# An expert stage's second product: one PSUM tile for both halves of a slot, or one for each

## The chip, the cores and the metric

The kernel runs on one core of a Trainium2 chip. The metric is the device time of one execution in microseconds (us). The engines of a core are TensorE (PE, matmuls; its weight loads are shown as PEld), VectorE (DVE), ScalarE (ACT), GpSimd (POOL) and SyncE (SP). Matmuls write to PSUM, ACT and DVE read it from there into SBUF, DMAs move data between SBUF and device memory (HBM).

## The reference

The input is first filtered along the sequence by a Fourier transform, then goes through a three-way maxout layer, and at last through a layer of eight experts of which each token uses one:

```python
# 1: filter
X = np.fft.rfft(x, axis=1); y = np.fft.irfft(X * F, n=3072, axis=1)     # x: (8, 3072, 256)
# 2: maxout, on 24576 tokens of 256 numbers, inner width 768
x = np.maximum(np.maximum(y @ w1, y @ w2), y @ w3) @ w_out
# 3: experts, inner width 1024
logits = xn @ en.T / tau;  expert_idx = np.argmax(logits, axis=1)        # 8 experts
for e in range(E):
    mask = expert_idx == e
    h = np.maximum(x[mask] @ w1[e], 0.0)
    out[mask] = gate_w[mask, None] * (h @ w2[e])
```

The change touches the last line alone, `h @ w2[e]` and the multiplication by the gate.

## The kernel before

All matmul operands are split into a high and a low part (`split`), and each product is the sum of three matmuls (high by high, high by low, low by high), so that the sum is near float32. `mm` (L214) issues every such matmul.

The program has two parts that follow each other. In the first, up to about 2115 us, filter and maxout run interleaved; its results (`pso` from `x2_tile`, evicted in three ACT instructions on L579 to L585) go to HBM as the table `x2d`, and each token's place in a list by expert is written (`route1` to `route3`).

In the second part, the expert stage, the lists are cut into *slots* of 256 tokens, all of one expert. 103 slots are built, of which the first 100 run in the generator `slots` and the last three stand in a branch that is taken only if they are needed; with this input 100 run. For each slot `s`:

- `w_load` (L1061) fetches the expert's weights into one of three buffers (`w` stands for two of them, `wt` for the third), an indirect DMA on POOL's queue; rows of an expert that is there already are skipped. `x_load` (L1106, POOL's queue) gathers the tokens three slots ahead, `x_turn` (L1118, SP's queue) transposes them by DMA, and `x_split` makes `xT`: two copies (ACT L1126, DVE L1127), then the high part on ACT (L217) and the low part on DVE (L218).
- `up(s, j)`, `j` from 0 to 3, is a quarter of the first product: two of the eight blocks of 128 inner features, 6 matmuls of 256 columns a block, 12 in all, into a PSUM tile `psh` of a pool of five. ACT makes `h`'s high part (L1148), DVE its low part (L1149).
- `down(s, t)`, `t` 0 and 1, is the second product for the first or second 128 tokens of the slot: 24 matmuls into `pso3` (shown as `pso`), over all eight blocks of `h`. Then ACT multiplies by the gate and evicts to `o` (L1165).
- `o_store(s)` scatters the two halves of `o` to the output (L1170, POOL's queue).

The order on every engine is that in which the code issues (a manual schedule; no scheduler moves anything). `slots` goes through its steps so: up(s,0), up(s,1), down(s-1,0), x_split(s+1), up(s,2), down(s-1,1), then the output's stores and the loads and transposes for later slots, up(s,3). So 12 matmuls of the first product stand between the two halves of the second, and 36 between the second half and the next slot's first half. The last step has no `up`: there the two halves of the last slot follow each other directly.

`pso3` comes from the PSUM pool `pf` (L231) with three buffers, each of one bank (2 KB a partition); that pool also serves the filter and the routing. One tile of 2 by 256 float32 fills a buffer. The build makes an instruction wait for an earlier one on another engine if both use the same tile and one writes.

Of the kernel before, what the change touches and what calls it, by code (L numbers as in the profile page):

```python
# [10 lines left out]
F32 = mybir.dt.float32  # L11
# [5 lines left out]
ACTF = mybir.ActivationFunctionType  # L17
# [3 lines left out]
NB, SEQ, D = 8, 3072, 256  # L21
# [161 lines left out]
def fft_filter_maxout_moe_kernel(ctx: ExitStack, tc: tile.TileContext, I, out):  # L183
# [4 lines left out]
    pe, act, dve, pool, sp = nc.tensor, nc.scalar, nc.vector, nc.gpsimd, nc.sync  # L188
# [24 lines left out]
    def mm(o, l, r, start, stop):  # L213
        pe.matmul(out=o, lhsT=l, rhs=r, start=start, stop=stop)  # L214
# [5 lines left out]
    def body():  # L220
        st = ExitStack()
        with st:
            def mk(name, bufs, **kw):
                return st.enter_context(tc.tile_pool(name=name, bufs=bufs, **kw))
# [3 lines left out]
            m1_p, m2_p, h_p = mk("m1", 2), mk("m2", 2), mk("h", 8)  # L228
            mk("gap", 1).tile([128, 32], F32, name="gap")
            gs_p, r_p, rt_p = mk("gs", 2), mk("r", 1), mk("rt", 2)  # L230
            pp, pf = mk("pp", 5, space=PSUM), mk("pf", 3, space=PSUM)  # L231
# [560 lines left out]
            for j in range(2):  # L792
                for k in range(2):
                    for w in range(3):
                        key = (w, k, j)
                        sc = slice(WM * 384 * j, WM * 384 * (j + 1))
                        c = slice(384 * j, 384 * j + 384)
# [300 lines left out]
            xg, xT, hs, ot = {}, {}, {}, {}  # L1098
# [32 lines left out]
            def parts(s, i):  # L1131
                t = ws[BUF[s]][i]
                return (
                    t.rearrange("p (a c d) -> p a c d", a=2, c=8) if i
                    else t.rearrange("p (a k c m) -> p a k c m", a=2, k=2, c=8)
                )
# [16 lines left out]
            def down(s, t):  # L1153
                w, g = parts(s, 1), gates[s]
                if t == 0:
                    ot[s] = (
                        m1_p.tile([128, 2, D], F32, tag="m1", name="o"),
                        pf.tile([128, 2, D], F32, tag="pf", name="pso3"),
                    )
                o, ps = ot[s]  # L1160
                for f in range(8):
                    h = hs[s, f // 2]
                    for i, (a, c) in enumerate(((0, 0), (0, 1), (1, 0))):
                        mm(ps[:, t], h[:, a, f % 2, 128 * t:128 * t + 128], w[:, c, f], f + i == 0, f == 7 and i == 2)
                act.activation(out=o[:, t], in_=ps[:, t], func=ACTF.Copy, scale=g[:, t].bitcast(F32))  # L1165

            def o_store(s):
                o = ot.pop(s)[0]
                for t in range(2):
                    d = pool.indirect_dma_start(  # L1170
                        out=out, out_offset=bass.IndirectOffsetOnAxis(ap=slot[s][:, t], axis=0),
                        in_=o[:, t], in_offset=None, bounds_check=NTOK - 1, oob_is_err=False,
                    )
                    tc.declare_no_dep(d.ins, group="out", reason="every row is written once")
                    tc.add_to_no_dep_group("out", d.ins)

            def slots(first, end):

                for s in range(first, end + 1):
                    on, near = s < end, first < s < end - 1  # L1180
                    if s == first:
                        w_load(AFTER.get(s - 1, 4), 0)
                        w_load(AFTER.get(s - 1, 4), 1)
                    for j in range(4):
                        if on:
                            up(s, j)
                        if j in (1, 2):
                            if on:
                                yield
                            if s > first:  # L1190
                                down(s - 1, j - 1)
                        if j == 1 and near:
                            x_split(s + 1)
                        if j == 2:
                            if s > first:
                                o_store(s - 1)
                            if s + 2 < end:
                                x_turn(s + 2)
                            if s + 3 < end:
                                x_load(s + 3)  # L1200
                            if s > first and AFTER.get(s - 1, end) < end:
                                w_load(AFTER[s - 1], 1)
                        if j == 3 and AFTER.get(s, end) < end:
                            w_load(AFTER[s], 0)
                        yield
# [40 lines left out]
            for x in range(18 * 49):  # L1246
                u, pt = divmod(x, 18)
                fc, w = divmod(pt, 3)
# [101 lines left out]
```

## Time and profile before

| what | us |
|---|---|
| three runs | 3310.49, 3314.74 (median), 3317.52 |
| the profiled execution, its own time | 3308.4 |
| its span, first to last instruction | 3306.6 |
| PE busy in the span | 3176.2 (96%) |
| last matmul starts, last eviction starts | 3295.77, 3296.09 |

The profiled execution's time is 1.8 us more than its span. A busy time of PE counts a matmul from its start to its modelled end, and matmuls overlap, so a busy PE is not one at its peak. A name such as `pso` stands for the tile with the buffer's number left out; times in a timeline count from the span's start.

### The profile page before, as it was taken

The numbers are of one execution on the slowest core, as the hardware profiler recorded it, in microseconds if no ns is written. First come the engines' busy times: TensorE is split into PE (matmuls) and PEld (weight loads), VectorE is DVE, ScalarE is ACT, GpSimd is POOL, SyncE is SP. The second block draws the span as 40 slices with busy tenths as digits, with TensorE's granted clock in tenths as the row PEclk, the third lists the DMA queues.
The fourth block names the chain that finished last, engine by engine and source line by source line (L and its number), as shares of the span: only waits on it lengthen the run. The fifth ranks groups of instructions, "written<-read, shape, count | busy, mean of one in ns | idle before, by whom it ended". The sixth has DMA issues, their size and how long they took to land.

```text
span 3306.6 us, 57241 instructions
## 1 busy us (share of the span) xinstructions
PE 3176.2 (96%) x20524; PEld 2842.3 (86%) x20524; DVE 1920.5 (58%) x4313; ACT 1525.4 (46%) x3450; POOL 1252.1 (38%) x1310
## 2 busy tenths in 40 slices
PE   5899999999999999999999999989999999999998
PEld 2588888888888888888888878889999999999998
DVE  6678687786788756878657675433333333333332
ACT  3455555556555554554446554333333333333333
POOL 3233233232333322333222233255555555555553
PEclk6799999999999999999999999999999999999999
DMA  7756566566555442444217865324233445224234
GB/s 233 220 146 146 141 140 138 136 121 159 139 116 119 89 138 79 99 104 98 54 35 229 214 198 187 95 60 120 69 69 71 118 118 170 68 68 118 70 70 141
DMA packets 345346, 405.61 MB, mean 123 GB/s; under 512 B 169240, under 2 KB 253475, under 8 KB 342116
## 3 DMA queue, kind: packets, MB, share of 16 engines
q1 hardware_dynamic: 248756, 247.81, 31.8%
q0 software_dynamic: 55088, 103.76, 10.7%
q10 hardware_dynamic: 41216, 50.35, 4.7%
q8 instruction: 164, 2.69, 0.4%
q14 instruction: 122, 1.00, 0.1%
HBM read 613.61 MB, written 140.97 MB: 228 GB/s over the span
## 4 chain that ended last, share of the span: by engine, by line
PE 34%; issue 21%; POOL 14%; DVE 2%; DMA 1%; POOLq 1%; ACT 0%; another core or an unknown queue 0%; SPq 0%; ACTq 0%; DVEq 0%
PE p L214 22%; PE pso L214 8%; POOL out L1170 5%; POOL xg L1106 4%; POOL w L1061 4%; POOL wt L1061 2%; PE psy L214 1%; PE psi L214 1%; PE psb L214 1%; DMA gt<-s 1%; PE psa L214 1%; DMA xw<-xg 0%; POOLq L1170 0%; POOLq L1106 0%; POOLq L1061 0%
## 5 line engine op out<-in xcount | busy, mean ns | idle before, releaser
L214 PE MATMUL p<-y,wt 128*128 128x512 f32 x5184 | 1306.9, 396 | 6.4 <-DVE m L553 3.9
L214 PEld LDWEIGHTS p<-y,wt 128*128 128x128 f32 x5184 | 952.8, 189 | 200.0 <-DVE m L553 4.1
L1149 DVE SCALAR_TENSOR_TENSOR h<-psh,h 128x512 fp32r<-128x512 f32 x400 | 275.7, 689 | 408.5 <-ACT h L1148 277.1
L214 PEld LDWEIGHTS pso<-wo,h 128*128 128x128 f32 x3456 | 448.5, 190 | 19.8 <-ACT m L545 3.6
L214 PE MATMUL pso<-wo,h 128*128 128x264 f32 x3456 | 454.0, 286 | 3.2 <-ACT m L545 3.2
L214 PE MATMUL pso<-w,h 128*128 128x256 f32 x3264 | 410.8, 282 | 12.2 <-ACT o L1165 9.3
L214 PE MATMUL psh<-xT,w 128*128 128x256 f32 x3264 | 410.8, 280 | 8.7 <-DMA w<-wsd,wi 4.4
L214 PEld LDWEIGHTS pso<-w,h 128*128 128x128 f32 x3264 | 391.6, 189 | 24.4 <-ACT o L1165 24.4
L214 PEld LDWEIGHTS psh<-xT,w 128*128 128x128 f32 x3264 | 394.2, 190 | 10.2 <-issue 8.3
L398 POOL TENSOR_TENSOR t<-t,ft 96x256 f32<-96x256 f32 (+1 forms) x192 | 185.2, 966 | 557.8 <-issue 256.6
L1170 POOL DMA_INDIRECT out<-o,ti x200 | 200.8, 1004 | 448.9 <-ACT o L1165 440.0
L1148 ACT ACTIVATE h<-psh 128x512 fp32r<-128x512 f32 x400 | 237.3, 594 | 282.0 <-PE psh L214 252.6
L523 POOL TENSOR_TENSOR y<-df,sm 128x256 fp32r<-128x256 f32 x192 | 156.8, 817 | 485.8 <-DVE df L522 477.4
L676 POOL DMA_INDIRECT lst<-ids,pi x192 | 214.5, 1117 | 325.8 <-DVE gs L260 147.9
L1165 ACT ACTIVATE o<-pso,gate 128x256 f32<-128x256 f32 x200 | 94.8, 474 | 442.5 <-PE pso L214 434.0
L259 ACT ACTIVATE h<-m 128x512 fp32r<-128x512 f32 x288 | 181.4, 630 | 218.5 <-DVE m L553 200.6
L218 DVE TENSOR_TENSOR xT<-xf,xT 128x512 fp32r<-128x512 f32 x100 | 69.2, 692 | 363.7 <-ACT xT L217 291.6
L260 DVE TENSOR_TENSOR h<-m,h 128x512 fp32r<-128x512 f32 x288 | 210.7, 732 | 70.7 <-ACT h L259 67.0
L553 DVE TENSOR_TENSOR m<-p,m 128x512 f32<-128x512 f32 x288 | 197.4, 685 | 87.2 <-PE p L214 82.5
L549 DVE TENSOR_TENSOR m<-p,m 128x512 f32<-128x512 f32 x288 | 197.0, 684 | 72.1 <-PE p L214 63.0
L579 ACT COPY r<-pso 128x512 uint16<-128x512 uint16 x192 | 112.5, 586 | 259.0 <-PE pso L214 238.1
L1106 POOL DMA_INDIRECT xg<-x2d,ti x200 | 205.7, 1029 | 67.2 <-issue 62.9
(176 smaller groups left out, 4192.5 us busy)
## 6 DMA issues: line engine op xcount, KB each, us to landing
ft<-in_filt SPq DMA_DIRECT2D x192, 192.0 KB
wsd<-wsp SPq DMA_DIRECT2D x32, 1024.0 KB
x2d<-r SPq DMA_DIRECT2D x48, 514.0 KB
xt<-in_x SPq DMA_DIRECT2D x96, 256.0 KB
s<-ot ACTq DMA_DIRECT2D x96, 256.0 KB
gt<-s SPq DMA_DIRECT2D x94, 256.0 KB
bt<-bmd SPq DMA_DIRECT2D x320, 72.0 KB
raw<-in_e SPq DMA_DIRECT2D x32, 512.0 KB
```

Source lines behind the costliest of these rows:

```text
L214: pe.matmul(out=o, lhsT=l, rhs=r, start=start, stop=stop)
L259: act.activation(out=hi, in_=src, func=ACTF.Copy)
L260: later(1, lambda: dve.tensor_tensor(out=lo, in0=src, in1=hi.bitcast(F32), op=ALU.subtract))
L398: pool.tensor_tensor(out=t[:, w], in0=t[:, w], in1=by(ft, 1), op=ALU.mult)
L549: dve.tensor_tensor(out=m2, in0=ps, in1=m_t[u, fc], op=ALU.max)
L553: dve.tensor_tensor(out=m2, in0=ps, in1=m2, op=ALU.max)
L676: s = pool.indirect_dma_start(out=lst1, out_offset=bass.IndirectOffsetOnAxis(ap=pi[:, t:t + 1], axis=0), in_=ids[:, t:t + 1], in_offset=No ...
L1061: pool.indirect_dma_start(out=ws[BUF[s]][i].bitcast(F32), out_offset=None, in_=wsd[i], in_offset=bass.IndirectOffsetOnAxis(ap=cols["wi"][: ...
L1106: pool.indirect_dma_start(out=g[:, t], out_offset=None, in_=x2d[0:n], in_offset=bass.IndirectOffsetOnAxis(ap=slot[s][:, t], axis=0), bound ...
L1148: act.activation(out=h[:, 0], in_=ps, func=ACTF.Relu)
L1149: dve.scalar_tensor_tensor(out=h[:, 1], in0=ps, scalar=0.0, in1=h[:, 0].bitcast(F32), op0=ALU.max, op1=ALU.subtract,)
L1170: d = pool.indirect_dma_start(out=out, out_offset=bass.IndirectOffsetOnAxis(ap=slot[s][:, t], axis=0), in_=o[:, t], in_offset=None, bounds ...
```

## The change

Each call of `down` takes a tile of its own of 256 float32 from the pool, where before the first call took one of 2 by 256 for both calls. The output tile `o` in SBUF remains one for both.

```diff
             def down(s, t):
                 w, g = parts(s, 1), gates[s]
                 if t == 0:
-                    ot[s] = (
-                        m1_p.tile([128, 2, D], F32, tag="m1", name="o"),
-                        pf.tile([128, 2, D], F32, tag="pf", name="pso3"),
-                    )
-                o, ps = ot[s]
+                    ot[s] = m1_p.tile([128, 2, D], F32, tag="m1", name="o")
+                o = ot[s]
+                ps = pf.tile([128, D], F32, tag="pf", name="pso3")
                 for f in range(8):
                     h = hs[s, f // 2]
                     for i, (a, c) in enumerate(((0, 0), (0, 1), (1, 0))):
-                        mm(ps[:, t], h[:, a, f % 2, 128 * t:128 * t + 128], w[:, c, f], f + i == 0, f == 7 and i == 2)
-                act.activation(out=o[:, t], in_=ps[:, t], func=ACTF.Copy, scale=g[:, t].bitcast(F32))
+                        mm(ps, h[:, a, f % 2, 128 * t:128 * t + 128], w[:, c, f], f + i == 0, f == 7 and i == 2)
+                act.activation(out=o[:, t], in_=ps, func=ACTF.Copy, scale=g[:, t].bitcast(F32))
 
             def o_store(s):
-                o = ot.pop(s)[0]
+                o = ot.pop(s)
```

The pool's buffers keep their size, since its other tiles are of 2 by 256. A slot now takes two of the three in turn instead of one.

On PE, in a slot late in the stage, the end of the first half, the first product's third quarter and the second half stood so before (numbers tell tiles apart: `pso_38306` is the slot's output tile, the `h` are its four inner tiles):

```order
L214 MATMUL pso_38306<-w_21263,h_38267 128x256 x3
L214 MATMUL psh<-xT,w_24599 128x256 [waits PE_49]
L214 MATMUL psh<-xT,w_24599 128x256 x11
L214 MATMUL pso_38306<-w_21263,h_38140 128x256 [waits Activation_49]
L214 MATMUL pso_38306<-w_21263,h_38140 128x256 x5
L214 MATMUL pso_38306<-w_21263,h_38156 128x256 x6
L214 MATMUL pso_38306<-w_21263,h_38207 128x256 x6
L214 MATMUL pso_38306<-w_21263,h_38267 128x256 x6
```

and stand so in the changed kernel:

```order
L214 MATMUL pso_38392<-w_21263,h_38353 128x256 x3
L214 MATMUL psh<-xT,w_24599 128x256 [waits PE_49]
L214 MATMUL psh<-xT,w_24599 128x256 x11
L214 MATMUL pso_38442<-w_21263,h_38225 128x256 x6
L214 MATMUL pso_38442<-w_21263,h_38241 128x256 x6
L214 MATMUL pso_38442<-w_21263,h_38292 128x256 x6
L214 MATMUL pso_38442<-w_21263,h_38353 128x256 x6
```

The matmuls stand in the same order; the second half writes another tile, and its first matmul no longer waits for ACT.

On ACT, from the first half's eviction to the second's, another slot near the end, before:

```order
L1165 ACTIVATE o<-pso_39620,gate 128x256 [waits DMASW5_49,DMASW4_49,PE_49]
L1126 COPY xf<-xw 128x2x2x128 [waits DMAHW7_49,DMAHW0_49]
L217 ACTIVATE xT<-xf 128x512 [waits DVE_49,Activation_49]
L1148 ACTIVATE h_39667<-psh 128x512 [waits PE_49]
L1165 ACTIVATE o<-pso_39620,gate 128x256 [waits PE_49]
```

and in the changed kernel, where the eviction's line is L1163:

```order
L1163 ACTIVATE o<-pso_39715,gate 128x256 [waits DMASW5_49,DMASW4_49,PE_49]
L1126 COPY xf<-xw 128x2x2x128 [waits DMAHW7_49,DMAHW0_49]
L217 ACTIVATE xT<-xf 128x512 [waits DVE_49,Activation_49]
L1148 ACTIVATE h_39762<-psh 128x512 [waits PE_49]
L1163 ACTIVATE o<-pso_39765,gate 128x256 [waits PE_49]
```

Here nothing moved and no wait changed; the second eviction reads another tile than the first.

## Rows read from the trace of the kernel before

**Rows 1.** The page: PE's busy share of 40 slices, and the granted clock.
```profile
PE   5899999999999999999999999989999999999998
PEclk6799999999999999999999999999999999999999
```

**Rows 2.** Busy time of each engine by stretch.
```profile
core 0: us, PE busy (x) PEld busy (x) DVE busy (x) ACT busy (x) POOL busy (x), PEclk, DMA share, GB/s
1100.00:1300.00 200.00, 200.00 (x1086) 171.50 (x1085) 120.50 (x279) 105.03 (x256) 46.70 (x55) 1.00 0.40 110
2135.80:2140.80 5.00, 5.00 (x26) 5.00 (x25) 0.69 (x1) 0.64 (x2) 1.64 (x2) 0.50 0.85 120
2300.00:2500.00 200.00, 196.88 (x1655) 193.54 (x1655) 65.25 (x120) 78.02 (x138) 104.26 (x104) 1.00 0.29 68
2500.00:2700.00 200.00, 196.27 (x1650) 192.93 (x1650) 65.83 (x121) 77.46 (x138) 104.60 (x104) 1.00 0.43 110
```

**Rows 3.** All waits of PE from 2190 us: total us, times, longest.
```profile
PE pso L214 <- ACT o L1165: 14.9, 55, 0.6
```

**Rows 4.** Tile pso, whole span: durations in ns, and who waited for it.
```profile
L214 PEld LDWEIGHTS pso<-w,h x3264: 186/188/330, 2121.6 to 3295.7; 128*128 128x128 f32 x192
...
L1165 ACT ACTIVATE o<-pso,gate x200: 468/474/477, 2124.9 to 3296.1; 128x256 f32<-128x256 f32 x100
...
  PEld pso L214: 37.0, 93
```

**Rows 5.** Timeline of two slots: start and length in us, [idle before <-releaser].
```profile
2501.72 2.99 PE L214 MATMUL pso<-wt,h 128*128 128x256 f32 x24
...
2504.55 1.54 PE L214 MATMUL psh<-xT,w 128*128 128x256 f32 x12
2505.70 0.47 ACT L1165 ACTIVATE o<-pso,gate 128x256 f32<-128x256 f32 x1 [3.18 <-PE pso L214]
...
2506.22 2.81 PEld L214 LDWEIGHTS pso<-wt,h 128*128 128x128 f32 x24 [0.33 <-ACT o L1165]
2506.22 3.01 PE L214 MATMUL pso<-wt,h 128*128 128x256 f32 x24
...
2507.53 0.69 DVE L218 TENSOR_TENSOR xT<-xf,xT 128x512 fp32r<-128x512 f32 x1 [3.85 <-ACT xf L1126]
...
2509.07 4.41 PE L214 MATMUL psh<-xT,w 128*128 128x256 f32 x36
...
2513.31 2.99 PE L214 MATMUL pso<-w,h 128*128 128x256 f32 x24
...
2516.14 1.54 PE L214 MATMUL psh<-xT,w 128*128 128x256 f32 x12
...
2517.81 3.10 PE L214 MATMUL pso<-w,h 128*128 128x256 f32 x24
...
2520.74 1.54 PE L214 MATMUL psh<-xT,w 128*128 128x256 f32 x12
...
2522.12 2.88 PE L214 MATMUL psh<-xT,wt 128*128 128x256 f32 x24
...
2524.84 2.99 PE L214 MATMUL pso<-w,h 128*128 128x256 f32 x24
```

**Rows 6.** Timeline, start of one second half: its first weight loads and matmuls.
```profile
2517.80 0.77 PEld L214 LDWEIGHTS pso<-w,h 128*128 128x128 f32 x6 [0.32 <-ACT o L1165]
2517.81 0.86 PE L214 MATMUL pso<-w,h 128*128 128x256 f32 x5
```

**Rows 7.** Timeline of the stage's end.
```profile
3282.81 1.11 PE L214 MATMUL pso<-w,h 128*128 128x256 f32 x8
...
3283.76 1.54 PE L214 MATMUL psh<-xT,w 128*128 128x256 f32 x12
3283.96 0.47 ACT L1165 ACTIVATE o<-pso,gate 128x256 f32<-128x256 f32 x1 [2.23 <-PE pso L214]
...
3285.14 2.99 PE L214 MATMUL pso<-w,h 128*128 128x256 f32 x24
...
3292.95 2.90 PEld L214 LDWEIGHTS pso<-w,h 128*128 128x128 f32 x24 [0.82 <-ACT o L1165]
```

## The prediction

> **What bounds the kernel now.** I read the page first. TensorE (PE) is busy 96% of the span and the granted clock stands at nearly full speed in almost every slice [rows 1], so time can only be won where PE stands still or spaces its matmuls wider. The change touches only the expert stage, the last third of the span. There the table by stretches shows PE busy 196 to 197 of each 200 us at granted clock 1.00, while VectorE (DVE) has work for 65, ScalarE (ACT) for 78 and GpSimd (POOL) for 104 us [rows 2]: PE is the bound and the others have room. A slot holds 96 matmuls of 256 columns (48 of the first product, 48 of the second); 1655 + 1650 of them in 400 us make 0.1210 us each, 11.62 us a slot.
>
> Next I asked what PE waits for in that stage. From 2190 us to the end the list of its waits has a single line: `pso`, the second product's output, waits for the ACT instruction `o` on L1165, which evicts that output [rows 3]. That line is small (14.9 us) because a PE row counts as idle only after the modelled end of the last matmul. The weight loads, which stand in the same queue, show it in full: 93 idle times before a `pso` load, 37.0 us, ended by `o` [rows 4].
>
> The timeline shows where. At 2501.72 the first half's 24 matmuls begin, at 2504.55 twelve `psh` matmuls of the next slot, and at 2505.93 (12 by 0.115) the second half should begin. It begins at 2506.22, its weight load after 0.33 us of idle time ended by `o` [rows 5]. That `o` evicts the *first* half; it reads other columns of the same PSUM tile, and the build orders the second half behind it.
>
> One more thing is to be seen. `o` takes 0.47 us [rows 4] and would be done long before the twelve matmuls are. But it starts only at 2505.70, although the first half's last matmul ends, as modelled, at 2504.71: 1.0 us late. In the last `slots` step that computes both products, where no gather, transpose or weight load for a later slot is issued any more, `o` starts at 3283.96, 0.04 us after the first half's end (3282.81 + 1.11), and the second half begins at 3285.14, 12 spacings behind 3283.76, with no idle time [rows 7]. So the late start, not the eviction's length, makes PE wait; why it is late the trace doesn't say.
>
> **The change, part by part.** *Removed:* the wait of each second half on the first half's eviction. The instruction order shows the twelve `psh` matmuls followed by the second half with no wait; nothing else on PE, and no instruction or DMA on any engine, moves.
>
> Price of one wait. Matmuls are spaced 0.118 us (2501.72 to 2504.55, 24 of them) [rows 5]. A weight load lasts 0.188 us [rows 4] and so normally overlaps the next by 0.07. A mean stop is (37.0 - 0.82) / 92 = 0.393 us of idle time, the 0.82 being the last slot's [rows 4, 7]; with the lost overlap, 0.464 us. The matmul rows agree: at 2517.81 the gap to the last `psh` (which starts 0.28 before 2516.14 + 1.54) is 0.41, 0.29 too long, and five matmuls then take 0.86 where 4 by 0.118 + 0.28 = 0.75 are normal, 0.11 more, since the second one waits for its weights; 0.40 together, against 0.32 + 0.07 for that slot's load [rows 5, 6].
>
> 92 stops by 0.464 are 42.7 us, and the last slot, where the two halves follow each other directly, gives 0.82 + 0.07. Sum: 43.6 us.
>
> Here a rule could shrink the price. The Trainium skill ("TensorE: Matmul & The Clock Gate", section "Architectural detail: the array is 16× 32×32, not 1× 128×128") says that PE's queue can pull a weight load ahead of matmuls in flight. By it the waiting half's weights would already be in, a stop would cost only the matmul's 0.35 us, and the sum would be 33 us. The trace disagrees: load and matmul start together at 2506.22.
>
> *A side effect on spacing.* Two spacings occur. The 36 `psh` matmuls from 2509.07 take 4.24 us (0.118); those from 2520.74 take 4.10, the 24 from 2522.12 at 0.113 [rows 5]. Behind an unstopped first half at 0.118 the `psh` matmuls go over to the shorter one (twelve from 2516.14: 1.54 - 0.28 over 11, 0.1145). If the second half runs unstopped like the first (2.83 us) and the 36 behind it like those of 2520.74, half and 36 take 6.93 us; now they take 7.09 (2506.22 to 2513.31) or 7.03 (2517.81 to 2524.84), while the delay of the first matmul is 0.464 - 0.11 = 0.35. That makes 0.45 to 0.51 a slot, 41 to 47 us in all. I take 45 us. Bounds: everything at 0.118 gives 96 by 0.118 = 11.33 against 11.62, 0.29 by 92, 27 us; everything at 0.113 gives 10.85, 71 us.
>
> *Added:* a second buffer per slot from a ring of three. The first half's tile is handed out again three halves later, to the next slot's second half: eviction over at 2506.17, next write at 2517.81 [rows 5]. That is 11.6 us of cover; if an eviction were later than this, PE would stop again. Cost: nothing.
>
> *What is late next.* With 0.46 us less per slot, the nearest input of PE is the next slot's `xT`: its low part is written by DVE at 2507.53 for 0.69 and is first read by the first product 12 spacings after 2509.07, at 2510.48 [rows 5]. 2.2 us are spare now, about 1.8 after. The late `o` stays, but only the store on POOL waits for it, and POOL is half empty [rows 2]. Expert weights and gathered rows come by DMA; PE waits for none after 2190 [rows 3], and the stage gets 4% shorter around them.
>
> Sum against the profiled execution: 3308.4 - 45 = 3263.4 us. It ran 6.3 us under the median of the runs shown (3314.74), so for a median I say 3269 us.
>
> **Rivals.**
> 1. *The long spacing stays everywhere.* For it: after a stop the half sometimes runs at once at the short one (3.01 - 0.11 us for 24 from 2506.22), so stops may be one way into it. Against: the unstopped 2520.74 shows the short one too. Gain 27 us: 3288.
> 2. *The wait moves to another input* (`xT`, weights, the ring), or the second half keeps its wait because both tiles count as one. For it: the order of the rows is fixed, and each is needed once a slot. Against: the spare times above, and the order of the changed kernel, which shows the wait gone. Gain near nothing: 3315.
> 3. *Slower: the granted clock falls*, now that PE never pauses. At clock 0.50 (2135.80 to 2140.80, the 1.2 GHz level) 26 matmuls take 5 us, 0.19 each against 0.118 [rows 2], though some records may be missing. Each one at the lower level costs about 0.08 us; some 560 of them, six slots' worth, use up the 45 us. From there on it decides; nine slots' worth gives 3339. Against: from 1100 to 1300 PE is busy 200 of 200 us at clock 1.00 [rows 2].
> 4. *The short spacing spreads:* up to 71 us, say 60: 3254.
>
> **How the numbers follow.** Forecast 0.75 (3260 to 3278, the price bounds of 36 to 50 us and a few us between runs); rival 1 0.12; rival 2 0.05; rival 3 0.03; rival 4 0.05. The range 3256 to 3288 leaves out rivals 2 and 3, and part of rival 4. About 0.2%, 6.6 us, is what a measurement of this kernel can tell from no change: faster 0.92, same 0.05, slower 0.03.
>
> **What would show it.** Right: in the changed profile no PE wait on L1163's `o` after 2190; no weight load idle before `pso`; about 4% more matmuls in 200 us of that stage (some 1720); `o` of the first half still 1 us behind its matmuls; the same tail behind the last matmul, earlier by the sum. Wrong: 48 `psh` matmuls per slot all at 0.118 (rival 1); a new line in PE's waits of some 0.4 us per slot (rival 2); a clock under 1.00 between 2200 and 3200 (rival 3). A gain far off with none of these would mean that the stops overlap something I haven't seen.

## The result, and the profile after

The changed kernel takes 3262.33 us (median of 4 runs, 3259.17 to 3274.65) where the kernel before takes 3312.61 us (4 runs, 3309.33 to 3317.52): a ratio of 0.9852, 95% interval 0.9833 to 0.9872. The profiled execution took 3259.17 us, its span is 3257.3 us.

The page of the changed kernel, PE's busy share and the granted clock in 40 slices, as in [rows 1]:

```profile
PE   5799999999999999999999999989999999999998
PEclk6799999999999999999999999989999999999999
```

The table by stretches, as in [rows 2]:

```profile
core 0: us, PE busy (x) PEld busy (x) DVE busy (x) ACT busy (x) POOL busy (x), PEclk, DMA share, GB/s
2300.00:2500.00 200.00, 200.00 (x1727) 200.00 (x1726) 68.65 (x126) 81.52 (x144) 109.14 (x108) 1.00 0.34 72
2500.00:2700.00 200.00, 200.00 (x1727) 200.00 (x1726) 68.89 (x126) 81.51 (x144) 108.98 (x108) 1.00 0.46 113
```

All waits of PE from 2190 us to the end, as in [rows 3]:

```profile
PE psh L214 <- DVE xT L218: 0.3, 1, 0.3
PE psh L214 <- ACT xT L217: 0.2, 1, 0.2
```

The tile `pso`, as in [rows 4]; no line for PE or its weight loads stands any more among those that waited for it, and this one leads that list:

```profile
L214 PEld LDWEIGHTS pso<-w,h x3264: 187/188/331, 2119.0 to 3246.3; 128*128 128x128 f32 x192
...
  POOL out L1168: 393.8, 193
```

The timeline of one slot, as in [rows 5], and below the three dots a place near the stage's end:

```profile
2496.55 2.99 PE L214 MATMUL pso<-w,h 128*128 128x256 f32 x24
...
2498.67 1.00 POOL L1061 DMA_INDIRECT w<-wsd,wi  x1 [0.30 <-issue]
...
2499.38 1.54 PE L214 MATMUL psh<-xT,w 128*128 128x256 f32 x12
2500.64 2.89 PEld L214 LDWEIGHTS pso<-w,h 128*128 128x128 f32 x24
2500.70 0.47 ACT L1163 ACTIVATE o<-pso,gate 128x256 f32<-128x256 f32 x1 [3.12 <-PE pso L214]
2500.76 2.99 PE L214 MATMUL pso<-w,h 128*128 128x256 f32 x24
...
2503.58 1.54 PE L214 MATMUL psh<-xT,w 128*128 128x256 f32 x12
2503.78 0.47 ACT L1163 ACTIVATE o<-pso,gate 128x256 f32<-128x256 f32 x1 [0.78 <-PE pso L214]
...
2504.96 2.88 PE L214 MATMUL psh<-xT,wt 128*128 128x256 f32 x24
...
2507.68 2.99 PE L214 MATMUL pso<-w,h 128*128 128x256 f32 x24
...
3216.40 0.48 DVE L1127 COPY xf<-xw 128x512 uint16<-128x512 uint16 x1 [5.47 <-DMA xw<-xg]
...
3217.89 0.38 PE L214 MATMUL psh<-xT,w 128*128 128x256 f32 x1 [0.23 <-ACT xT L217]
```

What is to be seen: PE is busy for all of each 200 us, with 1727 matmuls where it had 1655 and 1650, so a slot of 96 takes 11.12 us for 11.62. The second half begins at 2500.76, twelve spacings behind 2499.38, while the first half's `o` starts only at 2500.70, 1.16 us behind the end of its matmuls (2496.55 + 2.99 = 2499.54). So `o` is as late as before; nobody on PE waits for it. The second half's `o` starts at 2503.78, 0.03 us behind 2503.75.

### The profile page after: what moved, and what is told of

Its sections match the earlier page's. It is cut to its first block, busy times and chain, and to the rows that moved or that the text cites. A ratio compares the mean times of both kernels' runs of the same rounds, so it can differ in the third digit from the quotient of the medians.

```text
span 3257.3 us, 57243 instructions
## 1 busy us (share of the span) xinstructions
PE 3147.6 (97%) x20524; PEld 2833.4 (87%) x20524; DVE 1920.9 (59%) x4313; ACT 1524.9 (47%) x3450; POOL 1251.5 (38%) x1310
## 4 chain that ended last, share of the span: by engine, by line
PE 53%; issue 10%; POOL 7%; DVE 2%; DMA 1%; ACT 0%; POOLq 0%; ACTq 0%; SPq 0%; DVEq 0%
PE p L214 22%; PE pso L214 17%; PE psh L214 9%; POOL out L1168 2%; POOL w L1061 2%; POOL xg L1106 2%; PE psi L214 1%; PE psy L214 1%; PE psb L214 1%; POOL wt L1061 1%; PE psa L214 1%; DMA gt<-s 1%; DMA w<-wsd,wi 0%; DVE t L388 0%; DVE m L549 0%
## 5 line engine op out<-in xcount | busy, mean ns | idle before, releaser
L1163 ACT ACTIVATE o<-pso,gate 128x256 f32<-128x256 f32 x200 | 94.8, 474 | 392.4 <-PE pso L214 344.6
```

## Experiments

The change removes a wait on an eviction that would be no wait if it started on time. The main theory was: PE stops because `o` starts about 1 us late, on a late word from TensorE, and the tile of its own hides that. (By the instruction order the first half's `o` waits for two DMA queues too. In the kernel before, ACT passes that wait at 2501.9 in 38 ns, while the `o` behind it starts at 2505.70 [rows 5]; what is late is TensorE's word.) Rivals: the shared tile costs PE a stop whenever `o` comes, late or not; or it is the transposes, the weight loads or their bytes that make `o` late, and moving those would do as well. Each kernel was timed against the kernel before on its own chip. The records number the chips of the experiments, not that of the result above: the first four experiments ran on chip 5, the next four on chip 11, the last four on chip 1.

| run | chip | us, median | before there | ratio, 95% interval |
|---|---|---|---|---|
| e1_apart | 5 | 3290.92 | 3311.69 | 0.9933, 0.9907 to 0.996 |
| e2_loads_first | 5 | 3316.92 | 3311.69 | 1.0014, 1.0001 to 1.0027 |
| e3_no_transpose | 5 | 3303.5 | 3311.69 | 0.9973, 0.9961 to 0.9984 |
| e4_no_weight_loads | 5 | 3248.88 | 3311.69 | 0.9807, 0.9789 to 0.9824 |
| e5_small_loads | 11 | 3245.08 | 3250.99 | 0.9989, 0.9975 to 1.0003 |
| e6_adjacent | 11 | 3333.21 | 3250.99 | 1.0261, 1.0235 to 1.0287 |
| e7_own_adjacent | 11 | 3249.55 | 3250.99 | 0.9992, 0.9975 to 1.001 |
| e8_own_no_loads | 11 | 3242.54 | 3250.99 | 0.9977, 0.9963 to 0.999 |
| e9_before_again | 1 | 3305.07 | 3304.69 | 1.0002, 0.9992 to 1.0011 |
| e10_after_again | 1 | 3264.16 | 3304.69 | 0.9866, 0.985 to 0.9883 |
| e11_own_adjacent_again | 1 | 3262.09 | 3304.69 | 0.9865, 0.9839 to 0.989 |
| e12_small_loads_again | 1 | 3304.04 | 3304.69 | 0.9996, 0.9986 to 1.0006 |

**Shared tile, halves further apart (e1).** 24 `psh` matmuls stand between the halves in place of 12; the stores and loads of the slot move along.

```diff
-                            if s > first:
-                                down(s - 1, j - 1)
+                            if s > first and j == 1:
+                                down(s - 1, 0)
...
+                        if j == 3 and s > first:
+                            down(s - 1, 1)
+                            o_store(s - 1)
```

Expected: 

> The kernel before with the shared tile, but the second half one step later, so that 24 instead of 12 matmuls of the first product stand between the halves (the output's stores and the later slots' gathers go with it). Theory (the wait on the late eviction is the whole cost): 24 by 0.115 = 2.8 us cover the 1.5 us from the first half's end to the eviction's end, no stop is left, 11.1 us a slot, the changed kernel's time, some 3262 us. Rival (the gain needs a bank for each half, because PE and ACT no longer meet in one): the stops may go, but the time stays nearer 3310.

Measured 3290.92 us: 21 us gained, less than half of what the change brings. The stretch 2300 to 2500, and one slot of the timeline:

```profile
2300.00:2500.00 200.00, 198.80 (x1687) 196.86 (x1686) 68.29 (x123) 79.91 (x141) 105.92 (x105) 1.00 0.32 71
```

```profile
2503.11 2.99 PE L214 MATMUL pso<-w,h 128*128 128x256 f32 x24
...
2505.94 2.90 PE L214 MATMUL psh<-xT,w 128*128 128x256 f32 x24
2507.05 0.48 ACT L1165 ACTIVATE o<-pso,gate 128x256 f32<-128x256 f32 x1 [3.14 <-PE pso L214]
...
2507.80 1.02 POOL L1170 DMA_INDIRECT out<-o,ti  x1 [0.32 <-ACT o L1165]
...
2508.68 3.15 PE L214 MATMUL pso<-w,h 128*128 128x256 f32 x24
...
2509.84 1.78 PEld L214 LDWEIGHTS pso<-w,h 128*128 128x128 f32 x15 [0.15 <-issue]
2509.95 1.09 ACT L1148 ACTIVATE h<-psh 128x512 fp32r<-128x512 f32 x2 [1.10 <-PE psh L214]
```

The stop on `o` is gone, since `o` starts at 2507.05, late by 0.95 us, and is over long before 2508.68. But the second half has a pause inside it, at 2509.84, that waits for nothing the profile shows, and 24 matmuls take 3.15 us for 2.99; two evictions `h` of the first product, the earlier of which waited for PE, begin 0.11 us later. Time is thus still lost where nothing waits for the shared tile. The `h` are late as `o` was: the 24 `psh` end at 2508.84, the first `h` starts 1.11 us behind them, and POOL's issue of the output's store ends at 2508.82. That this lateness also makes the pause isn't shown; why the second half pauses here and not in the changed kernel stays open.

**POOL's issues in another order (e2).** The gather of `x` is issued behind the weight loads instead of ahead of them.

```diff
-                            if s + 3 < end:
-                                x_load(s + 3)
...
+                        if j == 3 and s + 3 < end:
+                            x_load(s + 3)
```

Expected: 

> The kernel before with one order changed on POOL's queue: the two weight loads of a slot go ahead of the two gathers, so weight loads issue 2.6 us earlier and the gathers (and the transposes that follow their landing) 2.6 us later. Theory L1 (the weight loads' issue makes PE's signal late): no PE signal falls in their time any more, the eviction starts 0.03 us behind the half, the stops shrink to nothing or to under 0.1 us, some 3265 to 3275 us. L2 (the transposes make it late): the first half's end still falls among them, stops stay, some 3310 us. L3 (neither): stays, some 3310 us.

Measured 3316.92 us, no faster. One slot:

```profile
2506.95 2.99 PE L214 MATMUL pso<-w,h 128*128 128x256 f32 x24
...
2508.95 1.01 POOL L1106 DMA_INDIRECT xg<-x2d,ti  x1 [0.30 <-issue]
...
2511.00 0.47 ACT L1165 ACTIVATE o<-pso,gate 128x256 f32<-128x256 f32 x1 [3.15 <-PE pso L214]
...
2511.52 1.56 PEld L214 LDWEIGHTS pso<-w,h 128*128 128x128 f32 x13 [0.40 <-ACT o L1165]
```

`o` starts 1.06 us behind the half's end (2509.94), although the last thing that POOL issued is now a gather of `x`. What it carries makes no difference here; that an issue ends (2509.96) just as the half ends is the same as before.

**No transposes (e3).** A plain copy replaces the transposing DMA, so `xw` holds untransposed rows.

```diff
-                    sp.dma_start_transpose(out=xw[s][:, t], in_=xg[s][:, t, 0:2 * D])
+                    sp.dma_start(out=xw[s][:, t].rearrange("p a b -> p (a b)"), in_=xg[s][:, t, 0:2 * D])
```

Expected: 

> The kernel before with a plain DMA copy of the same bytes in place of each DMA transpose; the tokens then reach the experts in another layout, so the output isn't the reference's. L1 (weight loads): the first half's eviction still starts 1.0 us late, some 3310 us. L2 (transposes): it starts on time, no stop, some 3265 us.

Measured 3303.5 us, 8 us less, but the tile's list of those that waited still has the stops in full, so the transposes aren't the cause:

```profile
  PEld pso L214: 43.9, 92
```

**No weight loads for later slots (e4).** The two calls of `w_load` in the slots' loop are left out of the kernel before; later slots multiply by old weights.

```diff
-                            if s > first and AFTER.get(s - 1, end) < end:
-                                w_load(AFTER[s - 1], 1)
-                        if j == 3 and AFTER.get(s, end) < end:
-                            w_load(AFTER[s], 0)
```

Expected: 

> The kernel before without the weight loads of later slots: every slot uses the weights of the first ones, so the output isn't the reference's. L1 (weight loads): the eviction starts on time, no stop, some 3260 to 3265 us. L2 (transposes) or L3 (neither): 1.0 us late as before, some 3310 us.

Measured 3248.88 us. The table by stretches, and one slot:

```profile
2300.00:2500.00 200.00, 200.00 (x1727) 200.00 (x1727) 68.50 (x126) 81.15 (x145) 73.19 (x72) 1.00 0.29 72
```

```profile
2496.42 1.03 POOL L1106 DMA_INDIRECT xg<-x2d,ti  x1 [0.30 <-issue]
...
2496.93 2.99 PE L214 MATMUL pso<-w,h 128*128 128x256 f32 x24
...
2499.75 1.54 PE L214 MATMUL psh<-xT,wt 128*128 128x256 f32 x12
2499.95 0.48 ACT L1165 ACTIVATE o<-pso,gate 128x256 f32<-128x256 f32 x1 [2.23 <-PE pso L214]
...
2501.14 2.99 PE L214 MATMUL pso<-w,h 128*128 128x256 f32 x24
```

`o` starts 0.03 us behind 2499.92, and the second half follows with no stop, with the shared tile: 1727 matmuls, as in the changed kernel. POOL's last issue ended at 2497.45, 2.5 us earlier. This shows the late `o` as the cause of the stops, and ties it to POOL's issues. Not all of the 63 us gained are stops: from 2120 to 2190 us PE has 551 matmuls here and 428 in the changed kernel, some 14 us of work at the 0.116 us of the changed kernel's slot, so that part lies at the stage's start.

**The same loads with few bytes (e5 and e12, one kernel on two chips).** The loads keep their number, place and waits, and carry 16 numbers a row in place of 4096, so later slots use old weights here too.

```diff
-                                w_load(AFTER[s - 1], 1)
+                                w_load(AFTER[s - 1], 1, 16)
...
-                            w_load(AFTER[s], 0)
+                            w_load(AFTER[s], 0, 16)
```

Expected on chip 11: 

> The kernel before, with the later slots' weight loads cut to 16 numbers a row instead of 4096: as many instructions on POOL's queue, a 256th of the bytes; the weights are then wrong for most slots, so the output isn't the reference's. If it is the number of loads on POOL's queue that makes PE's signal late: eviction 1.0 us late, about 0.46 us of stop per slot, some 3300 to 3312 us. If it is their size: eviction 0.03 us behind the half, no stops, 3249 us as without any load, at most 3262.

Expected on chip 1: 

> The kernel before with the later slots' weight loads cut to 16 numbers a row, as many instructions and waits as before (later slots' products use stale weights). Where the kernel before takes near 3310: if the bytes of the loads make the signals late, the time falls to about 3250 (0.981) and o starts within 0.1 us; if the instructions that issue the loads or their semaphores do, it stays within 3295 to 3315 with o about 1 us late. Where the kernel before takes near 3250 it tells nothing: 0.997 to 1.001.

Chip 11, 3245.08 us:

```profile
2496.31 2.99 PE L214 MATMUL pso<-w,h 128*128 128x256 f32 x24
...
2498.42 1.00 POOL L1061 DMA_INDIRECT w<-wsd,wi  x1 [0.30 <-issue]
...
2499.13 1.54 PE L214 MATMUL psh<-xT,wt 128*128 128x256 f32 x12
2499.33 0.48 ACT L1165 ACTIVATE o<-pso,gate 128x256 f32<-128x256 f32 x1 [2.23 <-PE pso L214]
...
2500.51 2.99 PE L214 MATMUL pso<-w,h 128*128 128x256 f32 x24
```

Chip 1, 3304.04 us:

```profile
2499.95 2.99 PE L214 MATMUL pso<-wt,h 128*128 128x256 f32 x24
...
2502.06 1.00 POOL L1061 DMA_INDIRECT wt<-wsd,wi  x1 [0.30 <-issue]
...
2504.11 0.47 ACT L1165 ACTIVATE o<-pso,gate 128x256 f32<-128x256 f32 x1 [3.37 <-PE pso L214]
...
2504.63 2.81 PEld L214 LDWEIGHTS pso<-wt,h 128*128 128x128 f32 x24 [0.52 <-ACT o L1165]
```

On chip 1 the bytes change nothing: `o` is 1.17 us late (2502.94 to 2504.11) and the time is that of the kernel before. The bytes are not the cause; the issuing is what is left. And the same instructions in the same order, with POOL's issue ending 0.12 us behind the half's end in both slots (2499.42 to 2499.30; 2503.06 to 2502.94), give `o` 0.03 us behind on chip 11. There the kernel before itself takes 3250.99 us (25 runs), 54 to 62 us less than on chips 1 and 5 and in the result above.

**The two halves back to back (e6 shared, e7 and e11 in tiles of their own).**

```diff
-                            if s > first:
-                                down(s - 1, j - 1)
+                            if s > first and j == 2:
+                                down(s - 1, 0)
+                                down(s - 1, 1)
```

Expected of e6: 

> The kernel before (one tile) with no matmul of the first product between the two halves, so that nothing covers the wait. Theory (the wait on the late eviction is the cost): the second half starts 1.5 us after the first half's end instead of right behind it, a stop of 1.7 + 0.1 us in place of 0.46, 92 times 1.3 more, some 3430 us; if the signal comes on time in this order, a stop of 0.65 to 0.85 us, some 3330 to 3350. Rival (what counts is the bank, not the wait): no change, some 3310.

Expected of e7: 

> The changed kernel (a tile for each half) in that same order, both halves back to back. Theory: no wait is left that the order could expose, 96 matmuls by 0.116 us a slot as in the changed kernel, some 3255 to 3270 us. Rival (two evictions close together, or a ring of three, stop PE): a new wait of pso on o, over 3280 us.

Expected of e11: 

> Each half in a tile of its own, and the two halves back to back. A slot has one change between pso and psh fewer than in the changed kernel, so about 0.03 us less a slot (11.10 for 11.13), 3 us over the stage: 0.999 of the changed kernel if nothing waits, on any chip. If late signals are there, the eviction of the first half (0.47 us) and then of the second start 1 us late, and pso's two tiles are wanted again a slot later, so no wait. Rival: with late signals TensorE pauses as it did with the second half moved apart (0.26 us a slot), and the time is 20 to 25 us above the changed kernel.

e6 took 3333.21 us on chip 11. One slot:

```profile
2509.45 2.99 PE L214 MATMUL pso<-w,h 128*128 128x256 f32 x24
...
2512.47 0.47 ACT L1165 ACTIVATE o<-pso,gate 128x256 f32<-128x256 f32 x1 [1.27 <-PE pso L214]
2513.00 2.89 PEld L214 LDWEIGHTS pso<-w,h 128*128 128x128 f32 x24 [0.77 <-ACT o L1165]
```

`o` is on time (2512.44 to 2512.47) and the second half still stands for 0.77 us, the eviction's 0.47 and what lies around it. So the wait of the shared tile is real on this chip too; the twelve `psh` matmuls in the kernel before hide it there. (3333.21 lies in the range that was named for an `o` on time, 3330 to 3350, by luck: that range was counted from 3310 us. From this chip's 3250.99 the same stop gives 3311 to 3329; measured are 82 us, some 0.9 us for each of 92 slots.) With tiles of their own the same order costs nothing: 3249.55 us on chip 11, and on chip 1 3262.09 us with

```profile
2300.00:2500.00 200.00, 200.00 (x1730) 200.00 (x1730) 68.63 (x127) 81.76 (x144) 109.36 (x108) 1.00 0.32 73
```

1730 against 1727 matmuls, 0.02 us a slot, fits the fewer changes between `psh` and `pso`. Beside the changed kernel on that chip (3264.16) that can't be told from no difference; no version with the right output is measurably better.

e11 also shows what happens on chip 1 when the half's end moves away from POOL's issue while every load stays:

```profile
2497.50 5.81 PE L214 MATMUL pso<-w,h 128*128 128x256 f32 x48
...
2498.28 0.99 POOL L1061 DMA_INDIRECT w<-wsd,wi  x1 [0.30 <-PE psh L214]
...
2500.52 0.47 ACT L1163 ACTIVATE o<-pso,gate 128x256 f32<-128x256 f32 x1 [1.07 <-PE pso L214]
```

The 24th of these 48 matmuls ends at 2500.48, POOL's last issue ended 1.2 us before it (2499.27), and `o` starts 0.04 us behind the half. So the loads alone don't make `o` late. Counted over the 100 first halves of a trace, "near" being an end within 0.2 us of the end of a POOL issue, and "late" an `o` more than 0.5 us behind:

| trace | chip | near | near and late | late, not near |
|---|---|---|---|---|
| before | not recorded | 94 | 93 | 0 |
| e10, changed kernel | 1 | 88 | 88 | 4 |
| e12, small loads | 1 | 92 | 90 | 2 |
| e11, halves back to back | 1 | 0 | 0 | 6 |
| e4, no weight loads | 5 | 1 | 0 | 1 |
| e5, small loads | 11 | 90 | 0 | 0 |

**The changed kernel without weight loads (e8)**, with the cut of e4.

Expected: 

> The changed kernel without the weight loads of later slots (each slot uses the weights of the first ones, so the output isn't the reference's). Without the loads the kernel before has no stops left and takes 3249 us. Theory (a tile of its own is worth the stops and nothing else): 3249 us here too, within 0.2%. Rival (a bank for each half is worth something by itself): faster than that by 10 us or more.

3242.54 us on chip 11, with 1727 matmuls in 200 us, as e4 has with the shared tile on chip 5 and e5 with it on this chip (3245.08 us). Where `o` is on time the tile of its own has nothing to remove.

**The pair again on chip 1 (e9, e10).** No edit.

Expected of the kernel before: 

> The kernel before, unchanged, for a profile from whatever chip this is. Theory L (the wait is on an eviction that TensorE's signal starts about 1 us late, and only some chips are late): where the time is near 3310, o of the first half starts about 1 us after the last matmul of its half, some 92 weight loads of pso wait for o, and 200 us hold about 1652 matmuls; where the time is near 3250, o starts within 0.1 us, at most 10 weight loads wait, and 200 us hold 1727. Rival G (the chip is faster as a whole, by DMA or clock, and the wait is there on both): near 3250 the 92 waits are still there.

Expected of the changed kernel: 

> The changed kernel, unchanged. Theory L: 3240 to 3262 on any chip; against the kernel before a ratio of 0.983 to 0.987 where that runs near 3310, and of 0.998 to 1.001 where it runs near 3250. Rival G: a ratio of about 0.985 on both kinds of chip, so 3200 where the kernel before takes 3250.

3305.07 and 3264.16 us. The ratio 0.9866 (0.985 to 0.9883) repeats the result; the changed kernel is 2 us above the top of what was expected. Its trace shows where: at one slot near the end the transposed rows come late.

```profile
3221.36 0.46 DVE L1127 COPY xf<-xw 128x512 uint16<-128x512 uint16 x1 [10.31 <-DMA xw<-xg]
...
3222.82 6.00 PE L214 MATMUL psh<-xT,w 128*128 128x256 f32 x24 [5.01 <-ACT xT L217]
```

```profile
3222.80:3227.80 5.00, 4.83 (x21) 4.54 (x22) 2.68 (x4) 1.91 (x4) 2.04 (x2) 0.50 1.00 245
```

PE stands for 5.01 us, and the granted clock is at 0.50, the 1.2 GHz level, in the 5 us behind it, while the DMA engines are busy throughout.

## Why the prediction was right, and where it was not

*The bound and the wait.* Right. The wait on `o` is gone from PE's list, the weight loads no longer stand before `pso`, and matmuls rose to 1727 in 200 us (some 1720 were named).

*The price.* 45 us were forecast, from 0.45 to 0.51 us a slot. The slot went from 11.62 to 11.12, 0.50 us, 46 us over 92. Between the first and the last weight load of this group lie 1174.1 us before [rows 4] and 1127.3 after (2119.0 to 3246.3): 46.8 us. The other 2.5 of the 49.3 us between the two spans lie ahead of 2119 or behind the end, where the change does nothing. The spacing came out as worked out: second half and the 36 `psh` behind it take 2.82 + 4.10 = 6.92 us (2500.76 to 2507.68), 6.93 forecast.

*Weights ahead of a stop.* By the Trainium skill ("TensorE: Matmul & The Clock Gate", section "Architectural detail: the array is 16× 32×32, not 1× 128×128") the queue can pull a load ahead of matmuls in flight, which the prediction priced at 33 us and took the trace to refute. Measured are 46 us. But the trace has the wait for ACT at the weight load itself (93 waits of `PEld` [rows 4]), and load and matmul then start together [rows 5]; so the rule isn't refuted, it doesn't reach this stop. Where nothing waits, the load does run ahead, by 0.12 us (2500.64 to 2500.76).

*The late `o`.* It stayed late, as named: 1.16 us.

*What is late next.* The place was right, `xT`, and its size was off. The 1.8 us of spare time were read from a slot in the middle; near the end the transposes land later, and one slot waits: 0.2 us for ACT's part of `xT` and 0.3 for DVE's in the profile after, 5.01 us and a lower clock on chip 1. On chip 1 the group's first and last load lie 1135.3 us apart (2118.7 to 3254.0), 8 more than in the profile after. It is a loss of that size or less, once, not per slot.

*The rivals.* All four fell. The short spacing isn't lost (36 `psh` in 4.10 us), nor does it spread (24 `pso` in 2.82). The wait moved nowhere else but to that one slot. The clock is 1.00 in the stretches shown; where it fell on chip 1 it was behind a pause of PE, not from the lack of one.

*What the prediction took for granted.* It priced the lateness of `o` as something that belongs to the kernel. It belongs to the kernel and the chip. In the result above and on chip 1, `o` is late and the change takes off 50 and 41 us; on chip 5 `o` is late too, but the changed kernel was not run there. On chip 11 the shared tile costs nothing in this order: a kernel with shared tiles (e5) and one with own tiles (e8) both reach 1727 matmuls in 200 us, and own tiles with the halves adjacent are at 0.9992 (0.9975 to 1.001). The changed kernel itself was not run there, so that it gains nothing on such a chip is inferred. If so, the right number owes something to luck, the result having been timed where `o` is late. The stops aren't all that the chips differ in: back to back with own tiles the kernel has 1730 matmuls in 200 us on both, and takes 3249.55 us on chip 11 and 3262.09 on chip 1. From 2120 to 2190 us PE has 570 matmuls there at a granted clock of 1.00, and 447 here at 0.90.

*Still open.* Why `o` starts late. On the chips where it does, it goes with the end of a POOL issue: in the profile after, e2 and e12 an issue ends within 0.13 us of the half's end, and `o` starts 1.03 to 1.05 us after that issue (2499.67 to 2500.70; 2509.96 to 2511.00; 2503.06 to 2504.11). With no issue near, by leaving the loads out (e4) or by moving the half (e11), `o` is on time. So the word from TensorE and POOL's issuing seem to hinder each other on some chips. By what, and what differs on chip 11, isn't known.

## What to carry to other kernels

Two halves in one PSUM tile are tied: the second can't start until the first is evicted, and a few matmuls between them hide that only if the eviction starts on time. Where the ring has room, a tile for each half cost nothing here (3249.55 for 3250.99 us on chip 11, with the halves back to back) and makes the order robust, also against a late start that only some chips show. Look for such stops in the idle time of the weight loads, since the matmul row shows less than half of it [rows 3, 4], and time a change of this kind on more than one chip before calling its gain a property of the kernel.

## What was not expected of the hardware

- An eviction whose last wait is for a half's last matmul starts 0.03 us after it (e4), or about 1 us after it where a POOL DMA issue ends within 0.2 us of that matmul (93 of 94 first halves in the kernel before; none of 90 on chip 11).
- The same kernel takes 3250.99 us on one chip and 3304.69 and 3311.69 us on two others.
- The bytes of the loads don't matter for the late start: cut to 16 numbers a row, the time on chip 1 is 3304.04 for 3304.69 us.
- Matmuls of 256 columns have two spacings, 0.118 and 0.113 us, and in the changed kernel's slot they change places with the products: 24 `pso` take 2.82 us (0.118), the 36 `psh` behind them 4.10 (0.114).
